# Order of the first loads, of one weight split and of two small preparations in a fused attention and expert kernel

## The chip, the cores and the metric

The kernel runs on one core of one Trainium2 chip. The metric is the device time of one execution in microseconds. Before the change it is 847.42 us, the median of 3 runs (846.95 to 848.21).

## What is computed

The reference first does attention over 4 batches, 8 heads, 576 positions, 64 columns a head. A position sees only a band behind it: heads 0 to 3 the last 32 positions, heads 4 to 7 every fourth of the last 128. Its result x, 2304 tokens by 512, goes through 4 experts that are all computed and added with weights:

```
scores = q @ k.T / sqrt(64); scores = where(mask, scores, -1e9)
attn = exp(scores - max); attn = attn / (sum(attn) + 1e-9)
x = (attn @ v), heads side by side                # 2304 x 512
p = domain_probs / (domain_probs.sum(-1) + 1e-9)  # 2304 x 4
out = sum over e of p[:, e] * (relu(x @ w1[e]) @ w2[e])   # 512 -> 1024 -> 512
```

## The kernel before

Attention is cut into 24 steps of two groups each, 192 positions of one head pair a group. A step goes through stages: `s_qk` (scores, TensorE, line 308), `s_max` (VectorE), `s_sub` (GpSimd), `s_exp` (ScalarE), `s_sum` (VectorE), `s_norm` (GpSimd), `s_tr` (transposes, TensorE, line 369) and `s_av` (products with v, TensorE, line 389). The main loop runs in rounds n (line 831). In the first part a round does scores of one step, the v products of the step three before it and the transposes of the step two before it, in this order on TensorE. Steps 0 to 4 start in rounds 0 to 4, steps 5 to 9 in rounds 8 to 12, the others from round 16 on. `START` is round 7, the round of step 4's v products; `OPEN` is round 15. Until `START` each round ends with three or four dummy matmuls (`dummies`, line 759), which keep TensorE at work.

The experts are cut into 16 units u of 256 hidden columns. All products are in float32r, and operands are split into a high and a low part: `split` (line 128) lets ScalarE write the high part (line 129) and VectorE or GpSimd the low part (line 126), so a product is high-high, low-high, high-low (line 427 for the first layer, line 530 for the second). Units 0 and 1 of the first block of 768 tokens are done plainly (`plain`, in two halves of tokens), from round 7 on with two items of `experts` a round: a round with the first two products (A11 and A21 with B11), one with the other two (A12 and A22 with B21), then the second layer's three tiles (`mm2`), and the same for unit 1. `mm2` adds to the accumulator with the experts' shares `pn`, which `weigh` makes (transposes on TensorE, line 724, then VectorE, lines 727 to 735). All other units take a scheme with fewer products (`mm1_a`, `mm1_b`) that needs sums of w1 and of x.

What prepares operands stands in a list `queue`: `prepare` adds a generator, `step` runs the first one up to its next yield, and `need` runs it to the end at once. In rounds 8 to 14 low parts are held back until the next round begins or something is needed. `x_part` splits a part of x, `w1_split` the blocks of w1, `w2_late` the two halves of w2 (for unit 1 the low part is on GpSimd).

Loads are issued by SyncE in the order of the list `loads` (line 809). At each round's start `load_ready` issues from the list's head as long as `ready` allows; a load that is not ready holds up the ones behind it, except that w2 is passed over. A tile that reuses a place makes SyncE wait for the place's last reader, and what is behind it in SyncE's queue waits too. A "fence" is a memset of one column of the tile on VectorE, for which the transfer then has to wait; it holds SyncE until VectorE has come to that point of its own queue. There are three places for q/k pairs (`QKB`) and four for v (`VB`). Before the change q/k 3 and 4 and v 4 use room in the tile `lent`, which is the first accumulator's, so that all five steps' q, k and v and w1 0 are issued without waiting; q/k 5 is fenced at round 6 (`n > half`). v_s, q_s and k_s are the tiles in their own places; both w1 and w2 land in tiles called r.

Of the kernel before, what the change touches and what calls it, by code (L numbers as in the profile page):

```python
# [8 lines left out]
F32 = mybir.dt.float32  # L9
F32R = mybir.dt.float32r  # L10
# [3 lines left out]
WINDOW = 32  # L14
# [4 lines left out]
GB = 6  # L19
GS = GB // 2  # L20
GW = GB * QB
PACE = 10
GAP = 3
QKB = 3
VB = 4
# [24 lines left out]
def kernel(  # L50
# [11 lines left out]
    nc = tc.nc  # L62
# [3 lines left out]
    NT, DM = out.shape  # L66
# [3 lines left out]
    FU = 256  # L70
    FPE = F // FU
    NU = E * FPE
    TB = 768
# [60 lines left out]
    def w1_split(u):  # L134

        r = raw1[u]
        gh = wp.tile([128, 3, 2, 128], F32R, tag="g1h", name="g1h", bufs=2)
        gl = wp.tile([128, 3, 2, 128], F32R, tag="g1l", name="g1l", bufs=2)
        a11, a12 = r[:, 0:2, 0:128], r[:, 2:4, 0:128]
        a21, a22 = r[:, 0:2, 128:256], r[:, 2:4, 128:256]  # L140
        for i, a in enumerate((a11, a12, a22)):
            split(gh[:, i], gl[:, i], a, nc.gpsimd if u else nc.vector)
            a_op[u, ("A11", "A12", "A22")[i]] = (gh[:, i], gl[:, i])
            yield
        if u < 2:
            ah, al = (
                fp.tile([128, TH], F32R, tag=t, name=t)[:, :FU].rearrange("p (c f) -> p c f", c=2)
                for t in (("hh12", "hl12"), ("u2", "s5"))[u]
            )
            split(ah, al, a21, nc.gpsimd if u else nc.vector)  # L150
            a_op[u, "A21"] = (ah, al)

    def w1_sums(u):

# [85 lines left out]
    def attention(ap, xrp, pa):  # L240
# [22 lines left out]
                ap=[row, (two.offset - one.offset, 2), col],  # L263
            )

        lent = fp.tile([128, TB // 128, DM], F32, tag="acc_0", name="lent")
        room = [lent.rearrange("p t d -> p (t d)")]

        def take(*shape):
            size = shape[0] * shape[1]  # L270
            t, room[0] = room[0][:, :size], room[0][:, size:]
            return t.rearrange("p (a b) -> p a b", a=shape[0])

        def load_qk(gs, k_queue, apart, fence):
            if apart:
                q_s, k_s = take(2, GW), take(2, GW + WINDOW)
            else:
                q_s = ap.tile([128, 2, GW], F32, tag="q", name="q_s", bufs=QKB)
                k_s = ap.tile([128, 2, GW + WINDOW], F32, tag="k", name="k_s", bufs=QKB)
            if fence:  # L280
                nc.vector.memset(q_s[:, 0, :1], 0.0)
            nc.sync.dma_start(out=q_s, in_=both(qT, gs, GW))
            k_queue.dma_start(out=k_s, in_=both(kT, gs, GW + WINDOW))
            for k, g in enumerate(gs):
                qk_t[g] = (q_s[:, k], k_s[:, k])

        def load_v(n, gs, apart):
            if apart:
                t = take(2, GB * 64).rearrange("p j (i d) -> p j i d", i=GB)
            else:  # L290
                t = ap.tile([128, 2, GB, 64], F32, tag="v", name="v_s", bufs=VB)
            for k, (b, p, gi) in enumerate(gs):
                nc.sync.dma_start(
                    out=t[KB * k:KB * (k + 1)], in_=vw[b, p][:, :, gi * GB:(gi + 1) * GB, :]
                )
            v_of[n] = t
# [216 lines left out]
    def mm2(k, first, last, half, cs=None):  # L513
        u, m = k
        e = u // FPE % E
        if first and m not in acc_t:
            if m == NBL - 1:
                pools["late"]()
            acc_t[m] = pools["acc"].tile([128, TB // 128, DM], F32, tag=f"acc_{m}", name=f"acc_{m}")
        for i in range(TH // 128):  # L520
            at = half * (TH // 128) + i
            tt = m * (TB // 128) + at
            acc = acc_t[m][:, at, :]
            po = pools["m2"].tile([128, 512], F32, tag="m2", name="m2")

            cs = cs or (range(2) if half == 0 else (1, 0))
            for n, (c, low) in enumerate([(c, low) for low in range(2) for c in cs]):
                h = h_t[k, f"{c + 1}{half + 1}"][low][:, i * 128:(i + 1) * 128]
                for x, w in enumerate(w2_op[u, c][:2 - low]):
                    nc.tensor.matmul(  # L530
                        po, h, w, start=(n == 0 and x == 0), stop=(n == 3)
                    )
            if first:
                nc.vector.tensor_scalar(
                    out=acc, in0=po, scalar1=pn[:, tt, e:e + 1], scalar2=None, op0=ALU.mult
                )
            else:
                nc.vector.scalar_tensor_tensor(  # L538
                    out=acc, in0=po, scalar=pn[:, tt, e:e + 1], in1=acc,
                    op0=ALU.mult, op1=ALU.add,  # L540
                )
            if last:
                nc.sync.dma_start(out=out[tt * 128:(tt + 1) * 128, :], in_=acc)
            yield
# [98 lines left out]
    with tc.manual_schedule():  # L643
# [131 lines left out]
        for n, i, names in (  # L775
# [9 lines left out]
        qk_done = av_done = 0  # L785
        shares = []
        ready = {"w2": lambda u: u < 1 or (u - 1, 1) in w2_op}
        half = needed[0] + 1
        ready["qk"] = lambda m: (
            m < half  # L790
            or n > half and qk_done > (m - half if m < half + QKB else m - QKB)
        )
        ready["v"] = lambda m: (
            m <= VB or av_done > m - VB - (m <= 2 * VB) and (m <= needed[1] or m <= qk_done)
        )

        def load(what, m):
            if what == "qk":
                load_qk(steps[m], nc.sync if m else nc.scalar, QKB <= m < half, m == half)
            elif what == "v":  # L800
                load_v(m, steps[m], m == VB)
            elif what == "masks":
                load_masks()
            elif what == "probs":
                shares.append(load_probs())
            else:
                (fetch_w1 if what == "w1" else fetch_w2)(m)

        loads = [
# [21 lines left out]
        for n in range(at(len(steps) - 1) + 5):  # L831
            load_ready()
            if START < n < OPEN:
                flush()
                holding.add(n)
                step()
            else:
                flush()
                holding.clear()
            for k, order in enumerate(stages):  # L840
                for stage, after in order:
                    m = step_at.get(n - after, -1)
                    if m >= 0 and k == (m > needed[1]):
                        stage(m, steps[m])
                        av_done += stage == order[(1, 2)[k]][0]
            if n in step_at:
                qk_done += 1
            for i, names in when.get(n, ()):
                for name in names:
                    of = first_x if i < 2 else later  # L850
                    if name is None or name == "T2":
                        prepare(x_sums, i, of=of)
                    if name is not None:
                        prepare(x_part, i, name.upper(), of=of)
            place = 0 if n <= START or n >= OPEN else len(queue)
            queue[place:place] = first_x
            first_x.clear()
            if n == 6:
                prepare(w1_split, 0)
            if n == START:  # L860
                prepare(w2_late, 0)
                prepare(w1_split, 1)
            if n == START + 2:
                weigh(shares[0])
            if n == START + 5:
                prepare(w2_late, 1, soon=True)
            if n == OPEN:
                gate.add("open")
            if n < START:
                dummies(FILL if n in step_at else FILL + 1)  # L870
                step()
                if n > 4:
                    step()
                    step()
                continue
            if "open" not in gate:
                for _ in range(2):
                    if next(ffn) == "idle":
                        dummies(2)
                step()  # L880
                continue
            for _ in range(PACE if n in step_at else 4):
                full = next(ffn)
                step()
                if n <= OPEN + 1:
                    step()
                if len(queue) > 8:
                    step()
                elif len(queue) < 5 and not full:
                    step(later)  # L890
# [62 lines left out]
```

## Time and profile before

| | us |
|---|---|
| median of 3 runs | 847.42 |
| profiled execution | 849.45 |
| its span, first to last instruction | 847.6 |
| TensorE busy (matmuls) | 826.9 |
| VectorE busy | 479.7 |
| GpSimd busy | 386.4 |
| ScalarE busy | 314.9 |

The mean granted TensorE clock over the span is 0.986. A granted clock of 1.00 is 2.4 GHz and 0.50 is 1.2 GHz. In the rows, PE is TensorE's matmuls, PEld its weight loads, DVE VectorE, ACT ScalarE, POOL GpSimd, SP SyncE; L389 is line 389; a q behind an engine's name is its queue, which issues and waits. All times count from the span's start.

### The profile page before, as it was taken

How to read it: one execution, taken by the hardware profiler on the slowest of the kernel's cores; microseconds unless marked ns; L12 is line 12 of the kernel's file. 1: busy time of each engine (PE TensorE's matmuls, PEld its weight loads, DVE VectorE, ACT ScalarE, POOL GpSimd, SP SyncE). 2: the span in 40 equal slices, each digit the busy share in tenths (PEclk: the TensorE clock that was granted, in tenths of full speed). 3: DMA queues.
4: the chain of work that ended last, by engine and by line, in shares of the span. 5: the costliest groups of instructions: out<-in, count | busy, mean ns of one | idle time of the engine just before them, and what ended most of it. 6: DMA issues, size and time to landing. Idle time of an engine off the chain costs nothing.

```text
span 847.6 us, 15414 instructions
## 1 busy us (share of the span) xinstructions
PE 826.9 (98%) x6172; PEld 727.3 (86%) x6172; DVE 479.7 (57%) x1042; ACT 314.9 (37%) x753; POOL 386.4 (46%) x467
## 2 busy tenths in 40 slices
PE   6979999999999999999999999999999999999998
PEld 3767888888878888899899898898998998988986
DVE  4365666655586558755545545545555455455554
ACT  2433544544454444433233233242342242232321
POOL 3264667986777679831432332342341342242210
PEclk9699999999999999999999999999999999999999
DMA  8662433343233311410100100101101001010003
GB/s 229 168 192 69 136 110 124 97 128 90 89 109 94 95 50 51 135 40 26 50 26 26 51 25 26 50 26 40 35 26 50 26 26 50 25 36 16 1 26 124
DMA packets 46610, 59.15 MB, mean 70 GB/s; under 512 B 2873, under 2 KB 36025, under 8 KB 46539
## 3 DMA queue, kind: packets, MB, share of 16 engines
q1 hardware_dynamic: 46123, 57.75, 22.6%
q8 instruction: 48, 0.79, 0.4%
q10 hardware_dynamic: 416, 0.43, 0.1%
q14 instruction: 23, 0.19, 0.1%
HBM read 53.45 MB, written 4.72 MB: 69 GB/s over the span
## 4 chain that ended last, share of the span: by engine, by line
PE 91%; POOL 3%; DVE 3%; ACT 2%; issue 1%; POOLq 0%; DVEq 0%
PE m L530 45%; PE m1x L427 23%; PE m1y L427 17%; PE po L389 2%; PE wt L759 1%; PE sc L308 1%; PE pt L369 1%; POOL w2l L126 1%; POOL sm L336 1%; DVE acc L538 1%; DVE sm L322 0%; POOL xl_T L126 0%; ACT hh L445 0%; POOL g2l L126 0%; ACT sm L343 0%
## 5 line engine op out<-in xcount | busy, mean ns | idle before, releaser
L538 DVE SCALAR_TENSOR_TENSOR acc<-m,pn,acc 128x512 f32<-128x512 f32 x270 | 201.8, 749 | 136.4 <-PE m L530 136.3
L530 PE MATMUL m<-w2h,hh 128*128 128x512 f32 x576 | 228.0, 396 | 3.9 <-ACT w2h L129 1.2
L530 PE MATMUL m<-w2l,hh 128*128 128x512 f32 x576 | 226.3, 393 | 2.2 <-POOL w2l L126 2.2
L126 POOL TENSOR_TENSOR g2l<-r,g2h 128x256 fp32r<-128x256 f32 x116 | 84.6, 762 | 214.8 <-PE m L530 212.5
L530 PE MATMUL m<-w2h,hl 128*128 128x512 f32 x576 | 179.2, 392 | 0.0
L445 ACT ACTIVATE hh<-s 128x384 fp32r<-128x384 f32 x92 | 48.4, 526 | 236.1 <-DVE s L468 183.5
L530 PEld LDWEIGHTS m<-w2h,hh 128*128 128x128 f32 x576 | 108.5, 188 | 27.3 <-DVE acc L538 4.0
L530 PEld LDWEIGHTS m<-w2h,hl 128*128 128x128 f32 x576 | 108.7, 189 | 24.0 <-DVE hl L451 0.3
L530 PEld LDWEIGHTS m<-w2l,hh 128*128 128x128 f32 x576 | 108.6, 189 | 22.7 <-POOL w2l L126 3.0
L126 POOL TENSOR_TENSOR w2l<-r,w2h 128x512 fp32r<-128x512 f32 x60 | 78.5, 1329 | 75.7 <-ACT w2h L129 75.6
L126 POOL TENSOR_TENSOR g1l<-r,g1h 128x256 fp32r<-128x256 f32 x93 | 69.9, 777 | 66.5 <-ACT g1h L129 66.4
L487 DVE TENSOR_TENSOR s<-m1x,s 128x384 f32<-128x384 f32 x46 | 25.6, 557 | 101.0 <-PE m1x L427 97.3
L478 ACT ACTIVATE u<-m1x 128x384 f32<-128x384 f32 x46 | 22.6, 492 | 150.4 <-PE m1x L427 150.4
L451 DVE SCALAR_TENSOR_TENSOR hl<-s,hh 128x384 fp32r<-128x384 f32 x92 | 53.7, 583 | 27.8 <-ACT hh L445 27.8
L427 PE MATMUL m1x<-xh_T,g2h 128*128 128x384 f32 x152 | 51.5, 339 | 0.8 <-DVE s L468 0.8
L427 PE MATMUL m1x<-xl_T,g2h 128*128 128x384 f32 x152 | 51.1, 336 | 0.0
L427 PE MATMUL m1x<-xh_T,g2l 128*128 128x384 f32 x152 | 51.0, 336 | 0.0
L129 ACT ACTIVATE g2h<-r 128x256 fp32r<-128x256 f32 x120 | 40.8, 410 | 4.8 <-POOL r L164 4.8
L427 PE MATMUL m1y<-xl_B,g2h 128*128 128x384 f32 x124 | 41.7, 336 | 0.0
L427 PE MATMUL m1y<-xh_B,g2h 128*128 128x384 f32 x124 | 41.5, 335 | 0.0
L427 PE MATMUL m1y<-xh_B,g2l 128*128 128x384 f32 x124 | 41.4, 334 | 0.0
L129 ACT ACTIVATE w2h<-r 128x512 fp32r<-128x512 f32 x64 | 39.1, 620 | 0.0
(128 smaller groups left out, 1483.5 us busy)
## 6 DMA issues: line engine op xcount, KB each, us to landing
r<-w SPq DMA_DIRECT2D x64, 512.0 KB, 3.4
v_s<-vw SPq DMA_DIRECT2D x46, 192.0 KB, 5.7
k_s<-kT SPq DMA_DIRECT2D x21, 224.0 KB, 4.9
out<-acc SPq DMA_DIRECT2D x18, 256.0 KB, 2.0
q_s<-qT SPq DMA_DIRECT2D x22, 192.0 KB, 5.0
lent<-kT SPq DMA_DIRECT2D x2, 224.0 KB
lent<-qT SPq DMA_DIRECT2D x2, 192.0 KB, 4.7
lent<-vw SPq DMA_DIRECT2D x2, 192.0 KB
```

Source lines behind the costliest of these rows:

```text
L126: lo_eng.tensor_tensor(out=lo, in0=src, in1=hi.bitcast(F32), op=ALU.subtract)
L129: nc.scalar.activation(out=hi, in_=src, func=AF.Copy)
L308: nc.tensor.matmul(banks[swap][o:o + QB, i * KB:(i + 1) * KB], q_s[h, c0:c0 + QB], k_s[h, c0:c0 + KB], start=True, stop=True, skip_group_c ...
L336: nc.gpsimd.tensor_tensor(out=sm, in0=sm, in1=nm.unsqueeze(2).to_broadcast([128, 2 * GS, KB]), op=ALU.subtract,)
L389: nc.tensor.matmul(po[k][64 * j:64 * j + 64, o:o + QB], v_s[rows, j, 2 * i + half, :], ts_[rows, c:c + QB], start=True, stop=True,)
L427: nc.tensor.matmul(bank, w[:, k], x[:, k], start=(first and k == 0 and i == 0), stop=(last and k == 1 and i == 2), skip_group_check=True,)
L445: nc.scalar.activation(out=hi, in_=src, func=AF.Relu)
L451: nc.vector.scalar_tensor_tensor(out=lo, in0=src, scalar=0.0, in1=hi.bitcast(F32), op0=ALU.max, op1=ALU.subtract)
L478: nc.scalar.activation(out=u2, in_=x, func=AF.Copy)
L487: nc.vector.tensor_tensor(out=s5, in0=x, in1=s5, op=ALU.add)
L530: nc.tensor.matmul(po, h, w, start=(n == 0 and x == 0), stop=(n == 3))
L538: nc.vector.scalar_tensor_tensor(out=acc, in0=po, scalar=pn[:, tt, e:e + 1], in1=acc, op0=ALU.mult, op1=ALU.add,)
```

## The change

The first half's q, k and v go into their own rotating places, `lent` is gone, and `ready` follows the number of steps done (`qk_done`, `av_done`). The second v comes behind q/k 3 and 4 in the order in which loads get ready, v 0 comes ahead of q/k 3, v 3 (the fourth) is fenced at round 3 and q/k 5 at round 5 instead of 6. `w1_split` splits A21 as the second of four instead of the last, with a step of its own. `weigh` runs in round `START + 1` instead of `START + 2`, and unit 1's `w2_late` is put at the queue's head in round `START + 4` instead of `START + 5`.

```diff
@@ w1_split
-        for i, a in enumerate((a11, a12, a22)):
+        for i, (n, a) in enumerate((("A11", a11), ("A12", a12), ("A22", a22))):
             split(gh[:, i], gl[:, i], a, nc.gpsimd if u else nc.vector)
-            a_op[u, ("A11", "A12", "A22")[i]] = (gh[:, i], gl[:, i])
+            a_op[u, n] = (gh[:, i], gl[:, i])
             yield
-        if u < 2:
...
+            if u < 2 and i == 0:
...
+                split(ah, al, a21, nc.gpsimd if u else nc.vector)
+                a_op[u, "A21"] = (ah, al)
+                yield
@@ load_qk, load_v
-            if apart:
-                q_s, k_s = take(2, GW), take(2, GW + WINDOW)
-            else:
-                q_s = ap.tile([128, 2, GW], F32, tag="q", name="q_s", bufs=QKB)
-                k_s = ap.tile([128, 2, GW + WINDOW], F32, tag="k", name="k_s", bufs=QKB)
+            q_s = ap.tile([128, 2, GW], F32, tag="q", name="q_s", bufs=QKB)
             if fence:
                 nc.vector.memset(q_s[:, 0, :1], 0.0)
+            k_s = ap.tile([128, 2, GW + WINDOW], F32, tag="k", name="k_s", bufs=QKB)
...
+            t = ap.tile([128, 2, GB, 64], F32, tag="v", name="v_s", bufs=VB)
+            if fence:
+                nc.vector.memset(t[:, 0, 0, :1], 0.0)
@@ main
-        half = needed[0] + 1
-        ready["qk"] = lambda m: (
-            m < half
-            or n > half and qk_done > (m - half if m < half + QKB else m - QKB)
-        )
+        ready["qk"] = lambda m: m < qk_done + QKB and (m != needed[0] + 1 or n >= m)
         ready["v"] = lambda m: (
-            m <= VB or av_done > m - VB - (m <= 2 * VB) and (m <= needed[1] or m <= qk_done)
+            m < av_done + VB and (m <= needed[1] or m <= qk_done) and (m != VB - 1 or n >= m)
         )
...
-                load_qk(steps[m], nc.sync if m else nc.scalar, QKB <= m < half, m == half)
+                load_qk(steps[m], nc.sync if m else nc.scalar, m == needed[0] + 1)
...
-                load_v(m, steps[m], m == VB)
+                load_v(m, steps[m], m == VB - 1)
...
-            ("qk", 0), ("masks", 0), ("qk", 1), ("qk", 2), ("qk", 3), ("v", 0), ("qk", 4),
+            ("qk", 0), ("masks", 0), ("qk", 1), ("qk", 2), ("v", 0), ("qk", 3), ("qk", 4),
             ("v", 1), ("v", 2), ("v", 3), ("w1", 0), ("v", 4), ("qk", 5), ("probs", 0),
...
-            if n == START + 2:
+            if n == START + 1:
                 weigh(shares[0])
-            if n == START + 5:
+            if n == START + 4:
                 prepare(w2_late, 1, soon=True)
```

## Rows read from the trace of the kernel before

**Rows 1.** The page: engine busy times, and the DMA queues (packets, MB, share).
```profile
PE 826.9 (98%) x6172; PEld 727.3 (86%) x6172; DVE 479.7 (57%) x1042; ACT 314.9 (37%) x753; POOL 386.4 (46%) x467
...
q8 instruction: 48, 0.79, 0.4%
```

**Rows 2.** Waits of TensorE, whole span: us in total, times, longest us.
```profile
PE po L389 <- issue: 4.3, 2, 4.1
PE m L530 <- POOL w2l L126: 2.2, 2, 1.7
...
PE m L530 <- ACT w2h L129: 1.2, 1, 1.2
...
PE m L530 <- DVE acc L534: 1.0, 1, 1.0
```

**Rows 3.** Stretches: busy us (instructions) per engine, granted clock, DMA share, GB/s.
```profile
16.17:20.26 4.09, 0.00 (x0) 0.00 (x0) 2.05 (x15) 0.00 (x0) 1.66 (x2) 0.90 0.66 164
20.26:32.34 12.08, 12.08 (x181) 7.74 (x180) 3.06 (x8) 5.27 (x15) 1.83 (x2) 0.50 0.24 75
32.34:36.92 4.58, 4.24 (x16) 3.45 (x12) 2.59 (x4) 3.13 (x8) 1.01 (x1) 0.54 1.05 310
...
56.35:62.57 6.22, 2.81 (x6) 1.32 (x6) 1.57 (x2) 1.67 (x4) 4.56 (x4) 0.83 0.29 81
62.57:68.74 6.17, 6.17 (x65) 5.00 (x64) 3.35 (x7) 1.46 (x4) 1.78 (x2) 0.62 0.97 292
```

**Rows 4.** Timeline of TensorE's matmuls, 13 to 21 us: start, us, instructions.
```profile
13.01 0.78 PE L389 MATMUL po<-pts,v_s 64*64 64x32 f32 x40 [0.18 <-issue]
...
15.50 0.67 PE L389 MATMUL po<-pts,v_s 64*64 64x32 f32 x32
20.26 0.65 PE L389 MATMUL po<-pts,v_s 64*64 64x32 f32 x16 [4.09 <-issue]
```

**Rows 5.** DMA view: 0 to 10.3, 10 to 11, 0 to 17.4, 17 to 18, 23 to 24.
```profile
DMA packets 2822, 2.67 MB, mean 259 GB/s; under 512 B 193, under 2 KB 2822, under 8 KB 2822
...
q8 instruction: 1, 0.02, 7.3%
...
DMA packets 4376, 4.58 MB, mean 263 GB/s; under 512 B 322, under 2 KB 4375, under 8 KB 4375
...
q8 instruction: 1, 0.02, 8.5%
...
q8 instruction: 1, 0.02, 5.5%
```

**Rows 6.** Timeline of SyncE's queue, 7 to 29 us: DMA issues.
```profile
7.12 4.77 SPq L293 DMA_DIRECT2D v_s<-vw  x6
11.93 0.59 SPq L107 DMA_DIRECT2D r<-w  x1
...
27.88 0.37 SPq L282 DMA_DIRECT2D q_s<-qT  x1
```

**Rows 7.** Timeline of TensorE's matmuls, 5 to 16 us: scores and a transpose.
```profile
5.31 0.84 PE L308 MATMUL sc<-k_s,q_s 64*32 64x64 f32 x48
...
6.84 0.72 PE L308 MATMUL sc<-k_s,q_s 64*32 64x64 f32 x48
...
10.73 0.55 PE L369 MATMUL pt<-ident,sm 128*128 128x128 f32 x3 [1.76 <-POOL sm L358]
...
11.86 0.72 PE L308 MATMUL sc<-lent 64*32 64x64 f32 x48
...
14.85 0.72 PE L308 MATMUL sc<-lent 64*32 64x64 f32 x48
```

**Rows 8.** Timeline of GpSimd, 57 to 66 us.
```profile
57.16 1.01 POOL L126 TENSOR_TENSOR xl_B<-xr,xh_B 128x384 fp32r<-128x384 f32 x1
58.12 2.81 POOL L126 TENSOR_TENSOR w2l<-r,w2h 128x512 fp32r<-128x512 f32 x2
65.53 0.83 POOL L358 TENSOR_TENSOR sm<-sm,rc 128x384 f32<-128x384 f32 x1 [4.59 <-DVE rc L353]
```

More of the change, by code (lines that the diff above doesn't have):

```diff
@@ L140, in w1_split @@
         a21, a22 = r[:, 0:2, 128:256], r[:, 2:4, 128:256]
-        for i, a in enumerate((a11, a12, a22)):
+        for i, (n, a) in enumerate((("A11", a11), ("A12", a12), ("A22", a22))):
             split(gh[:, i], gl[:, i], a, nc.gpsimd if u else nc.vector)
-            a_op[u, ("A11", "A12", "A22")[i]] = (gh[:, i], gl[:, i])
+            a_op[u, n] = (gh[:, i], gl[:, i])
             yield
-        if u < 2:
-            ah, al = (
-                fp.tile([128, TH], F32R, tag=t, name=t)[:, :FU].rearrange("p (c f) -> p c f", c=2)
-                for t in (("hh12", "hl12"), ("u2", "s5"))[u]
-            )
-            split(ah, al, a21, nc.gpsimd if u else nc.vector)
-            a_op[u, "A21"] = (ah, al)
+            if u < 2 and i == 0:
+                ah, al = (
+                    fp.tile([128, TH], F32R, tag=t, name=t)[:, :FU].rearrange(
+                        "p (c f) -> p c f", c=2
+                    )
+                    for t in (("hh12", "hl12"), ("u2", "s5"))[u]
+                )
+                split(ah, al, a21, nc.gpsimd if u else nc.vector)
+                a_op[u, "A21"] = (ah, al)
+                yield
     def w1_sums(u):
@@ L264, in both, with load_qk @@
             )
[L266 to L274, printed above, removed]
-            if apart:
-                q_s, k_s = take(2, GW), take(2, GW + WINDOW)
-            else:
-                q_s = ap.tile([128, 2, GW], F32, tag="q", name="q_s", bufs=QKB)
-                k_s = ap.tile([128, 2, GW + WINDOW], F32, tag="k", name="k_s", bufs=QKB)
+        def load_qk(gs, k_queue, fence):
+            q_s = ap.tile([128, 2, GW], F32, tag="q", name="q_s", bufs=QKB)
             if fence:
                 nc.vector.memset(q_s[:, 0, :1], 0.0)
+            k_s = ap.tile([128, 2, GW + WINDOW], F32, tag="k", name="k_s", bufs=QKB)
             nc.sync.dma_start(out=q_s, in_=both(qT, gs, GW))
@@ L285, in load_qk, with load_v @@
                 qk_t[g] = (q_s[:, k], k_s[:, k])
[L287 to L291, printed above, removed]
+        def load_v(n, gs, fence):
+            t = ap.tile([128, 2, GB, 64], F32, tag="v", name="v_s", bufs=VB)
+            if fence:
+                nc.vector.memset(t[:, 0, 0, :1], 0.0)
             for k, (b, p, gi) in enumerate(gs):
@@ L518, in mm2 @@
                 pools["late"]()
-            acc_t[m] = pools["acc"].tile([128, TB // 128, DM], F32, tag=f"acc_{m}", name=f"acc_{m}")
+            acc_t[m] = pools["acc"].tile([128, TB // 128, DM], F32, name=f"acc_{m}")
         for i in range(TH // 128):
@@ L787 @@
         ready = {"w2": lambda u: u < 1 or (u - 1, 1) in w2_op}
-        half = needed[0] + 1
-        ready["qk"] = lambda m: (
-            m < half
-            or n > half and qk_done > (m - half if m < half + QKB else m - QKB)
-        )
+        ready["qk"] = lambda m: m < qk_done + QKB and (m != needed[0] + 1 or n >= m)
         ready["v"] = lambda m: (
-            m <= VB or av_done > m - VB - (m <= 2 * VB) and (m <= needed[1] or m <= qk_done)
+            m < av_done + VB and (m <= needed[1] or m <= qk_done) and (m != VB - 1 or n >= m)
         )
```

## The prediction

> **What bounds the kernel now.** I read the page first. TensorE is busy 98% of the span [rows 1], so the time is its own work plus the few places where it waits or runs slowly; anything that leaves it idle or half-clocked early moves the end one for one. The list of TensorE's waits comes next [rows 2]: the largest is 4.1 us ahead of an attention product (line 389) with no releaser, named "issue"; then come two waits for the low part of unit 1's w2 (2.2 us), one for its high part (1.2) and one for the first accumulator (1.0). The table of stretches puts them in place [rows 3]. From 16.17 to 20.26 TensorE does nothing. From 20.26 to 32.34 it is busy for all 12.08 us at a granted clock of 0.50, which is the lower level, 1.2 GHz; the clock was at the upper level before the gap and fell in it. It is back in the next stretch. From 56.35 to 62.57 TensorE is busy for only 2.81 of 6.22 us, the clock falls again, and the stretch to 68.74 has a mean of 0.62. So the first 70 us hold two holes, each with a tail at half clock, and the change touches what stands around both.
>
> What is the first hole? TensorE's timeline shows it in the middle of one step's value products: 32 matmuls of 48, the gap, 16 more [rows 4]. Both halves of that step's v had been read before the gap, so it is no data wait. From the short "issue" gap before 13.01 to the large one TensorE issues 40 products, three transposes, three dummies, 48 scores [rows 7] and 32 products, 126 matmuls and as many weight loads, some 252 instructions. The page's instruction queue q8 brings 48 packets of together 0.79 MB [rows 1], one per 257 of TensorE's 12,344 instructions. I read the hole as TensorE out of instructions, at the end of such a block. The packet that ends it runs in 17 to 18 us [rows 5], and TensorE resumes at 20.26.
>
> Why so late? By 10.3 us 2.67 MB had moved, and the packet before started there; by 17.4 us it was 4.58 MB [rows 5]. From the tile shapes a q/k pair is 0.43 MB, a v pair 0.39, masks 0.20, one w1 tile 0.52. Five q/k pairs, masks and the first v, all that SyncE had issued by 7.1 us [rows 6], make 2.72 MB. With three more v pairs, w1 0 (11.93) and part of the last v, right behind it, it is about 4.6. Twice an instruction packet starts when the bytes issued some 3 to 5 us before it are through: it seems to stand in line behind them.
>
> **The change, part by part.** All sums are against the profiled execution, 849.45 us (span 847.6 and 1.85 around it). That lies 2.03 above the median of 847.42, and I take savings off the median.
>
> *The order of the loads.* q/k pairs 3 and 4 now reuse the places of pairs 0 and 1, so SyncE waits for the score blocks at 5.31 and 6.84 to end [rows 7], and v 1, v 2 stand behind that; v 3 waits for a memset on VectorE ahead of the fourth scores; w1 0 and v 4 follow. SyncE takes some 0.4 us to issue a q or k transfer (27.88) and 0.8 a v half (4.77 for six) [rows 6]. That gives: pair 3 issued at 6.2 to 7, pair 4 to 8.4, v 1 and v 2 to 11.6, v 3 at 11.9 to 13.5, w1 0 after that. Nothing of it is late for its reader. At (4.58-2.67)/7.1 = 0.27 MB/us pair 3 (2.3 MB in line) is through near 9 and pair 4 (2.7) near 10.4, their score blocks start at 11.86 and 14.85 [rows 7], and v 1 (3.1 MB) is through near 12 for a reader at 15.50. The memset costs VectorE one tiny operation; behind it stand only the scores, which come later.
>
> When TensorE asks for the block (12 to 13 us), 3.5 to 3.9 MB are in line rather than 4.4 or more. At 0.27 MB/us the packet starts at 13.4 to 14.9 instead of about 17.4, so 2.5 to 4 us sooner, and the 4.09 us hole shrinks to 0.1 to 1.6. I take 0.9: **-3.2** (from -4.1 to -2.4).
>
> *The clock.* With a hole of 0.9 us I expect the clock to stay up, as it did over the 1.76 us wait before 10.73 [rows 7]. The two rounds and a half in 20.26 to 32.34 then run at full clock. Halving all of the 12.08 busy us gives -6.0, the best end. The other end is the softmax chain: a round with scores took 2.99 at full clock (11.86 to 14.85) [rows 7], so 1.4 for the cut round, twice 2.99 and 0.9 for the last products make 8.3, and -3.8. The rounds in question have no scores; at 2.6 each the stretch is 7.5 us: **-4.6**. The two expert products in 32.34 to 36.92 hold 4.24 busy us at 0.54, so 2.3 at full clock. 0.34 of the stretch is idle, ahead of A21's product; splitting A21 second, on ScalarE and VectorE a round sooner, hides that behind the attention rounds, and if that cover is gone the 0.34 returns. 4.58 becomes 2.3: **-2.3** (from -2.6 to -1.9).
>
> *What TensorE runs into when it is ten microseconds early.* The second batch of loads (fenced at round 5 instead of 6) is issued from about 18.4, when VectorE is through round 4, not from 27.88 [rows 6]. Instruction blocks now stand behind it while TensorE drains them sooner. No row shows a wait there. Below it is 0; the upper bound is the hole itself, 4.1. By the same line-up I get blocks landing 0 to 1 us late at two or three places; I take **+2.0**.
>
> *Shares a round sooner.* Four transposes, a copy, and four small operations on VectorE move ahead of the first hidden layers' low parts. The 1.0 us wait for the first accumulator [rows 2] can go; but VectorE then does w2's low part, scores, shares and two hidden parts in a row. Between -1.0 and the same the other way; I take **0**.
>
> *Unit 1's w2 a round sooner.* GpSimd does this low part in 2.81 us, behind an x part of 1.01 us that starts at 57.16 [rows 8], and TensorE reads it at once. After the change its first half is through a round earlier, and its second, some 1.4 us, follows the softmax step that GpSimd leaves at 57.16: 58.6 rather than 60.9. Of 3.41 idle us in 56.35 to 62.57 some 1.6 remain. That is -1.8, and -0.5 for the clock in that stretch (2.81 busy at 0.83): **-2.3** (-3.9 if no wait is left, -0.5 if the w2 tile arrives late). With the wait halved I expect no second fall: 6.17 busy us at 0.62 are 3.8, **-2.3** (0 if it falls all the same). ScalarE's and GpSimd's x parts of chunk 0 come two steps later in turn: two of 1.01 us, hidden in GpSimd's idle time of 4.59 us before 65.53 [rows 8]; **+0.3**, at most +2.0.
>
> The sum: -3.2 -4.6 -2.3 +2.0 +0 -2.3 -2.3 +0.3 = -12.4, so 847.4 - 12.4 = **835.0**. All best ends (-4.1 -6.0 -2.6 +0 -1.0 -3.9 -2.3 +0) give -19.9 or 827.5, all bad ends (-2.4 -3.8 -1.9 +4.1 +1.0 -0.5 +0 +2.0) -1.5 or 846; as they hardly come together, the likeliest case alone runs from 829 to 842.
>
> **The rivals.**
>
> *The hole stays.* If an instruction packet does not stand behind data, the order of the data changes nothing: TensorE stops at the same place for 4.1 us and the clock falls. For this speaks that the bytes ahead were only bracketed, and that the packet of 23 to 24 us came about 3 us after TensorE resumed although the queues were empty [rows 5]; against it, the two starts that fit the line. Then A21's wait (0.34 idle and its tail at half clock, 0.6) and the second hole's -2.3 and -2.3 remain: 842. A page of the Trainium skill says just this: "DMA: Bandwidth & Descriptors", section "Queues, rings and completion order", has each DMA engine take turns between its queues packet by packet, so a lone instruction packet would be served at once. By that rule the result would be this rival's. The trace bears it out poorly (a start at 17.4 for a block asked for near 13), so it has 0.2.
>
> *The hole shrinks and the clock falls all the same.* A hole of 1.6 to 2.4 us plus waits in the softmax chain could be idle enough; the fall after 56.35 came with waits for w2 none of which was longer than 1.7 us [rows 2, 3]. Then only the hole's -2.4, A21's -0.6 and the second hole's -4.6 come: 840.
>
> *The hole moves.* This is the slower one. At 20 to 40 us the second batch, 3.1 MB, is issued at once, and TensorE's next blocks are asked for behind it. If one of them starts more than about 2 us after TensorE has used up the block before it, the clock falls in the middle of full expert work, where half clock costs half of the time: over 16 us, as long as it stayed low the first time (20.26 to past 32.34 and the tail), 8 us, and 4.1 for the hole. A residue of 1.6 in the first hole and the loss of the second hole's -4.6 to the same stall go with it: -10.1 +0.7 +4.1 +8 = +2.7, so 850. For it: 2.7 MB issued ahead put the first packet at 10.3, some 3 us after SyncE had issued them [rows 5, 6]. Against it: the batch is issued in three waits (for places), not in one.
>
> *It does not do what it says.* Gains early are given back because a later resource, GpSimd's x parts or a w2 load, sets the pace by 100 us: 847.
>
> **How the numbers follow.** Forecast 0.50 (835), hole stays 0.19 (842), clock falls 0.13 (840), hole moves 0.11 (850), given back 0.07 (847). 829 to 845.5 holds the forecast and the first two rivals nearly whole, about 0.8. A measurement of this kernel can tell 0.2%, 1.7 us, from no change: faster than 845.7 is 0.82, within 0.07, slower 0.11.
>
> **What would show it.** Right: the "issue" wait before line 389's products under 2 us, the instruction packet of that block starting before 15.5, granted clock 1.00 through 20 to 32, first expert product near 24.5 rather than 32.3, no wait over 1.2 us for w2's low part. The order of the loads is refuted if the packet still starts near 17.4; the clock step if the clock falls with a hole under 2 us; the part on w2 if TensorE still waits 3 us there. A new "issue" wait between 25 and 45 would be the third rival.

## The result and the profile after

The changed kernel takes 837.14 us (median of 4 executions, 834.86 to 839.03); the kernel before, run beside it, 847.18 (846.40 to 848.21). The ratio is 0.988, with a 95% interval from 0.985 to 0.991: 10.0 us faster. The profiled execution took 837.8 us with a span of 836.0, so span against span it is 11.6 us shorter. Line numbers of the changed kernel are 9 lower at the products: line 380 answers to 389, 360 to 369, 418 to 427, 521 to 530.

The page of the changed kernel, TensorE's busy time and granted clock:

```profile
PE 817.9 (98%) x6172; PEld 720.3 (86%) x6172; DVE 478.5 (57%) x1043; ACT 314.7 (38%) x753; POOL 386.3 (46%) x467
...
PEclk9999999999999999999999999999999999999999
```

The clock row of the kernel before:

```profile
PEclk9699999999999999999999999999999999999999
```

The number of matmuls is unchanged, VectorE has one instruction more, and the clock row no longer has the dip in its second slice. Of TensorE's waits over the whole span (us in total, times, longest) these lines answer to [rows 2]:

```profile
PE pt L360 <- issue: 2.1, 1, 2.1
...
PE m L521 <- ACT hh L436: 1.4, 3, 0.7
...
PE po L380 <- issue: 1.3, 1, 1.3
PE m L521 <- DVE acc L529: 1.2, 2, 0.8
PE m1x L418 <- DVE s L459: 1.1, 1, 1.1
...
PE m L521 <- POOL w2l L126: 0.9, 1, 0.9
...
PE m1y L418 <- issue: 0.6, 1, 0.6
```

The wait of 4.1 us before the products with v is 1.3. The wait for w2's high part is gone, that for its low part is 0.9 instead of 2.2. The wait for the accumulator at line 534 is gone too; the one at L529 stood in the kernel before as well. Two more rows of before:

```profile
PE m L530 <- DVE acc L538: 1.2, 2, 0.8
...
PE m L530 <- ACT hh L445: 0.3, 1, 0.3
```

New are a wait of 2.1 us without a releaser before a transpose and one of 0.6 before a first-layer product; the waits for hidden parts on ScalarE grew from 0.3 to 1.4.

The stretches of [rows 3], in the changed kernel, with a later one (columns as there):

```profile
16.17:20.26 4.09, 2.88 (x74) 2.16 (x74) 2.41 (x13) 1.84 (x6) 1.69 (x3) 1.00 1.07 229
20.26:32.34 12.08, 9.46 (x181) 7.12 (x178) 6.55 (x24) 6.44 (x18) 3.57 (x4) 1.00 1.08 265
32.34:36.92 4.58, 4.47 (x81) 3.37 (x89) 4.26 (x21) 2.50 (x7) 2.67 (x5) 1.00 1.08 224
36.92:53.00 16.08, 14.46 (x340) 11.90 (x329) 10.83 (x54) 7.98 (x20) 11.28 (x13) 1.00 0.72 212
```

The granted clock is 1.00 everywhere; before, TensorE did nothing in the first of them, and the next two had 0.50 and 0.54. The DMA share, which had sunk to 0.24 in the second, is above 1: the next batch of loads now runs here.

TensorE's timeline at the places that matter (start, us, instructions, idle before):

```profile
15.46 0.67 PE L380 MATMUL po<-pts,v_s 64*64 64x32 f32 x32
17.38 0.43 PE L380 MATMUL po<-pts,v_s 64*64 64x32 f32 x16 [1.25 <-issue]
...
24.51 0.33 PE L360 MATMUL pt<-ident,sm 128*128 128x128 f32 x1 [2.13 <-issue]
...
26.47 0.44 PE L418 MATMUL m1x<-xh_B,g1h 128*128 128x384 f32 x1
...
48.74 0.50 PE L521 MATMUL m<-w2h,hh 128*128 128x512 f32 x1 [0.45 <-ACT hh L436]
50.19 0.51 PE L521 MATMUL m<-w2l,hh 128*128 128x512 f32 x1 [0.95 <-POOL w2l L126]
...
73.83 0.50 PE L521 MATMUL m<-w2h,hh 128*128 128x512 f32 x1 [0.70 <-ACT hh L436]
74.82 0.50 PE L521 MATMUL m<-w2h,hh 128*128 128x512 f32 x1 [0.26 <-ACT hh L436]
...
83.34 0.44 PE L418 MATMUL m1x<-xh_T,g2h 128*128 128x384 f32 x1 [1.14 <-DVE s L459]
```

The first of these lines starts where its partner in [rows 4] does, and the stop falls after the same 32 of 48 products, as it would at the end of an instruction block. But it ends at 17.38 instead of 20.26.

Both kernels issue the same number of matmuls, 6172, in nearly the same order (the shares' four transposes move), so the start of one instruction in the two traces gives the lead at that point. Seven of them, and the end:

| instruction | before | after | lead |
|---|---|---|---|
| last 16 products after the first hole | 20.26 | 17.38 | 2.88 |
| first expert product | 32.34 | 26.47 | 5.87 |
| scores after the first two expert products | 36.93 | 28.75 | 8.18 |
| unit 1's last first-layer products (m1y, high part of B) | 55.04 | 46.54 | 8.50 |
| first v products after unit 1's first w2 round | 62.57 | 51.09 | 11.48 |
| first x part product behind that | 72.86 | 59.27 | 13.59 |
| first product with g2 | 95.25 | 83.34 | 11.91 |
| end of the span | 847.6 | 836.0 | 11.6 |

So 13.6 us were gained by 59 us, and 1.7 of them are given back between 59 and 83. From there to the end the two kernels run alike.

### The profile page after: what moved, and what is told of

Its sections match the earlier page's. It is cut to its first block, busy times and chain, and to the rows that moved or that the text cites. A ratio compares the mean times of both kernels' runs of the same rounds, so it can differ in the third digit from the quotient of the medians.

```text
span 836.0 us, 15418 instructions
## 1 busy us (share of the span) xinstructions
PE 817.9 (98%) x6172; PEld 720.3 (86%) x6172; DVE 478.5 (57%) x1043; ACT 314.7 (38%) x753; POOL 386.3 (46%) x467
## 4 chain that ended last, share of the span: by engine, by line
PE 92%; POOL 3%; DVE 2%; ACT 2%; issue 1%; POOLq 0%; DVEq 0%
PE m L521 45%; PE m1x L418 24%; PE m1y L418 17%; PE po L380 2%; PE sc L299 1%; PE pt L360 1%; PE wt L750 1%; POOL xl_T L126 1%; DVE acc L529 1%; POOL g1l L126 1%; ACT hh L436 1%; POOL w2l L126 0%; POOL g2l L126 0%; DVE sm L313 0%; ACT xh_T L129 0%
## 5 line engine op out<-in xcount | busy, mean ns | idle before, releaser
L529 DVE SCALAR_TENSOR_TENSOR acc<-m,pn,acc 128x512 f32<-128x512 f32 x270 | 201.8, 749 | 132.8 <-PE m L521 132.6
```

What stands on the lines that cost most here:

```text
L529: nc.vector.scalar_tensor_tensor(out=acc, in0=po, scalar=pn[:, tt, e:e + 1], in1=acc, op0=ALU.mult, op1=ALU.add,)
```

## The experiments

Runs e1 to e4, e5 to e8 and e9 to e12 shared a chip each, with the kernel before on it: 848.54, 847.79 and 847.08 (medians of 17, 11 and 11). The theory: instruction blocks of TensorE stand in line behind the data that was issued before them, so the loads' order sets the hole; a small hole keeps the clock up; the preparations remove the rest. The main rivals: instruction packets take turns with data and don't wait for it; the clock falls whatever the hole's size; the gain comes from the preparations alone.

**The loads alone, and the preparations alone.** e1 is the changed kernel with `w1_split` as before and the old rounds for the shares and w2:

```diff
-            if n == START + 1:
+            if n == START + 2:
                 weigh(shares[0])
-            if n == START + 4:
+            if n == START + 5:
                 prepare(w2_late, 1, soon=True)
```

> The changed kernel with A21 split last again, the shares at START + 2 and unit 1's w2 at START + 5 again: the change's loads alone. Theory (an instruction block stands in line behind the bytes issued before it): the order of the loads alone shrinks the first hole from 4.1 to about 1.2 us and keeps the clock up there, so the first expert product starts near 26.5 us rather than 32.3; the second hole stays as before, 3 to 3.4 us without work and a fall of the clock behind it. 839 to 841 us. Rival (turns: instruction packets do not stand behind data, and the gain is from the preparations): the hole stays at 4 us and the time at 847.

e2 is the kernel before with the new order of splits, shares and w2, its loads untouched.

> The kernel before with only A21 second, the shares and unit 1's w2 a round sooner; loads as before. Theory: first hole 4.1 us and half clock behind it as before; the second hole loses 2 to 3 us and, if the clock then stays up, 2 more: 841 to 843 us. Rival (turns): this is where the gain comes from, 837 to 838. If the w2 tile is what TensorE waits for rather than GpSimd's place in the order, 846 to 847.

Measured: e1 842.87 (841.37 to 843.66), ratio 0.993 [0.9916, 0.9945]; e2 843.35 (841.44 to 846.45), ratio 0.994 [0.9924, 0.996]. Either half brings some 5 us, 5.7 and 5.2; their sum of 10.9 lies between the two measurements of the whole, 10.0 above and 11.7 in e5. Both times are above what was expected (839 to 841, 841 to 843). In e1's waits the first hole is short and all of w2's stay:

```profile
PE m L518 <- POOL w2l L126: 2.2, 2, 1.7
PE pt L357 <- issue: 1.9, 1, 1.9
...
PE po L377 <- issue: 1.7, 1, 1.7
...
PE m L518 <- ACT w2h L129: 1.2, 1, 1.2
PE m L518 <- DVE acc L522: 1.1, 1, 1.1
```

In e1 the clock stays up to 55 us and falls only with the w2 waits (0.50 from 55.13 to 61.96). In e2 the first hole is the old one:

```profile
PE po L392 <- issue: 4.1, 1, 4.1
```

So the preparations don't touch the hole, and the loads don't touch w2. But part of e2's lead is the clock's. Behind this hole it came back after 3.4 us, where it stayed low until 36.5 us in the kernel before:

```profile
21.04:24.46 3.42, 3.42 (x61) 2.18 (x57) 0.91 (x3) 1.45 (x4) 0.05 (x1) 0.50 0.02 5
24.46:34.70 10.24, 8.69 (x195) 6.81 (x190) 3.55 (x7) 5.95 (x17) 2.79 (x3) 1.00 0.50 153
```

From the hole's end to the first expert product e2 takes 29.03 - 20.83 = 8.20 us instead of 12.08, in a stretch in which TensorE waits for nothing. No edit of e2 explains these 3.9 us, so how much of its 5.2 is the preparations' own is not shown, and that the halves add up proves little. e1 holds something else. Its timeline at A21's product:

```profile
28.74 0.44 PE L415 MATMUL m1y<-xh_B,hh 128*128 128x384 f32 x1 [0.51 <-ACT hh L129]
29.85 0.44 PE L415 MATMUL m1y<-xh_B,hl 128*128 128x384 f32 x1 [0.67 <-DVE hl L126]
```

TensorE waits 1.18 us for A21, where the kernel before is idle for 0.34 in that stretch [rows 3]: at half clock TensorE came to it more slowly, and ScalarE and VectorE nearly kept up.

**The line of bytes, first test.** e3 adds a load of 0.52 MB that nobody reads, on SyncE behind v 2:

```diff
-            ("v", 1), ("v", 2), ("v", 3), ("w1", 0), ...
+            ("v", 1), ("v", 2), ("extra", 0), ("v", 3), ("w1", 0), ...
```

> The changed kernel with one load more, 0.52 MB into the first accumulator's place, issued between v 2 and v 3; nobody reads it. Theory (line): at 0.27 MB a us the instruction packet of the first hole starts 1.9 us later, near 16.8 instead of 14.9, the hole grows from 1.25 to about 3.1 us, and the clock falls in it as before the change: 841 to 846 us. Rival (turns): the packet stays near 14.9, the hole at 1.25, the time at 837.

Measured: 839.58 (838.3 to 841.33), ratio 0.9895 [0.9877, 0.9913]. The packet came at 15.2 instead of 14.9 and the hole was 2.1 instead of 1.25; half clock from 18.15 to 21.56. The time is below the 841 to 846 expected. The direction of the hole is right, its size is not (3.1 was expected), and the trace says why: v 3 was issued at 11.93, behind the extra, and fell behind the packet. About 4.02 MB stood ahead instead of the 3.8 + 0.52 = 4.3 meant, so the added load pushed another out of the line. That alone doesn't separate the theories well; e12 does.

**The smallest cut of the line.** e4 is the kernel before with one edit, the fence on the fourth v:

```diff
+            if fence:
+                nc.vector.memset(t[:, 0, 0, :1], 0.0)
```

with `ready["v"]` holding v 3 until round 3.

> The kernel before, q/k 3 and 4 and v 4 still in the lent tile, with only the fourth v fenced at round 3, so that v 3, w1 0 and v 4 are issued from about 11.9 us on. Theory (line): of the bytes ahead of the block only those of w1 0 and part of the v's go; 3.5 to 3.9 MB in line, the packet at 14 to 15.5 us, a hole of 0.3 to 1.8, the clock up: 838 to 840 us with the second hole as before. If it takes the own places and their waits, or if only the total in the first 18 us counts: 847.

Measured: 845.22 (842.86 to 848.65), ratio 0.9967 [0.9951, 0.9982], 3.3 us faster, and not the 838 to 840 expected. The packet and the hole came as expected:

```profile
15.36 0.66 PE L391 MATMUL po<-pts,v_s 64*64 64x32 f32 x28 [0.36 <-DMA v_s<-vw]
17.05 0.43 PE L391 MATMUL po<-pts,v_s 64*64 64x32 f32 x16 [1.04 <-issue]
```

but the clock fell:

```profile
0.00:17.76 17.76, 13.13 (x366) 7.77 (x367) 9.04 (x73) 4.99 (x11) 7.93 (x16) 1.00 0.97 260
17.76:24.59 6.83, 6.83 (x108) 4.15 (x106) 1.96 (x5) 3.06 (x9) 2.05 (x3) 0.50 0.21 39
24.59:40.00 15.41, 13.22 (x250) 10.24 (x242) 8.99 (x41) 7.86 (x21) 5.44 (x7) 1.00 1.00 254
40.00:55.31 15.31, 11.12 (x234) 8.89 (x232) 10.71 (x52) 6.77 (x16) 9.80 (x12) 1.00 0.75 212
55.31:62.14 6.83, 6.47 (x62) 4.74 (x61) 2.59 (x6) 1.46 (x4) 2.25 (x3) 0.50 0.69 223
```

A hole of 1.04 us, less than the changed kernel's 1.25, was followed by 6.83 us at half clock. So the step "a hole of about 1 us keeps the clock up" is no law. In e4 scores at 34.85 waited 1.0 us for data besides, with the second batch of loads still fenced at round 6 as before the change, and products at 15.36 waited 0.4.

**The changed kernel again.** e5 is the changed kernel, unaltered.

> The changed kernel itself once more, beside the three that follow, since its executions spread over 4 us. Theory (line): packets start when the bytes issued ahead of them are through, so holes of 1 to 2 us near 17 and 22 us come again; how much of the clock is lost differs from execution to execution. About 0.988 of the time before: 837 to 839 us.

Measured: 836.07 (835.14 to 837.74), ratio 0.9866 [0.9849, 0.9883]. In its profile the holes are 1.5 and 0.8 us. The mean clock over the span was 0.997 to 1.0 in all eight executions of this kernel; in the kernel before it was 0.981 to 0.992 on this chip. So the second hole, 2.1 in one and 0.8 in the other, is a matter of one execution.

**The second batch later.** e6 fences q/k 5 at round 6, as before the change:

```diff
-        ... and (m != needed[0] + 1 or n >= m)
+        ... and (m != needed[0] + 1 or n > m)
```

> The changed kernel with q/k 5 fenced at round 6 instead of 5, so that the second batch is issued from about 20.5 us instead of 17.9. Theory (line): the packet that starts at 21.75 in the changed kernel, behind q/k 5, then has only the first batch ahead (4.8 MB) and starts near 19.5; the hole of 2.1 us ahead of the last transposes before the experts goes, the one of 0.6 at 32 may grow to 1; 835 to 837 us. Rival: the later batch makes scores or weights wait instead, no gain or up to 3 us slower than the changed kernel.

Measured: 838.23 (837.83 to 842.15), ratio 0.9887 [0.987, 0.9903]. The second hole is gone as expected, its packet running at 19.7 instead of 21.75, and a wait for data stands in its place:

```profile
PE sc L299 <- DMA k_s<-kT: 5.5, 2, 4.1
```

The profiled execution's clock was at 0.50 from 34.53 to 41.36 after that. So the outcome is the rival's. In the changed kernel the batch holds up instructions; issued later, it comes late itself.

**One part taken back at a time.** e7 puts w2 back to START + 5, e8 the shares back to START + 2, e9 A21's split back to the end of `w1_split`; all else is the changed kernel.

> The changed kernel with unit 1's w2 put at START + 5 again. Theory: TensorE waits for w2's parts for 3 to 3.4 us near 50 us and the clock falls for some us behind it: 3 to 5 us slower than the changed kernel, 840 to 843; and what the changed kernel gives back between 73 and 83 us (1.2 to 1.5 us, x parts two steps later) is not given back. Rival (data late or GpSimd's order does not matter): within 1 us of the changed kernel.

> The changed kernel with the shares at START + 2 again. Theory of the prediction: no difference, the wait of about 1 us for the first accumulator comes back and as much of the wait for the hidden layers' low parts goes; within 1 us of the changed kernel. Rival: the shares on VectorE ahead of the hidden parts cost nothing and the accumulator wait is pure gain: 1 us slower than the changed kernel.

> The changed kernel with A21 split last again. Theory: TensorE waits again before A21's product in the first expert round, 0.7 to 1.2 us as with the loads alone, nothing else moves: 0.7 to 1.5 us slower than the changed kernel, 837 to 838. Rival (hidden anyway): the same time.

| without | median (range) | ratio | what came back in the trace |
|---|---|---|---|
| w2 sooner (e7) | 838.98 (837.79 to 843.52) | 0.9908 [0.9887, 0.9928] | waits 1.2, 1.7 and 0.5 for w2; clock 0.50 from 49.83 to 56.66 |
| shares sooner (e8) | 837.67 (836.52 to 839.97) | 0.9885 [0.9869, 0.9901] | the accumulator's wait of 1.08 |
| A21 second (e9) | 838.51 (836.49 to 840.59) | 0.9893 [0.9874, 0.9912] | waits 0.50 and 0.67 for A21 |

Against the changed kernel's ratios, 0.988 [0.9851, 0.9908] here and 0.9866 in e5, the intervals overlap the wider one. Against e5, on the same chip, e7's does not, though its time is below the 840 to 843 expected; for the other two parts the times alone settle nothing. The rows say more. e8's line:

```profile
37.20 0.50 PE L521 MATMUL m<-w2h,hh 128*128 128x512 f32 x1 [1.08 <-DVE acc L525]
```

In e7's trace the first w2 product of unit 1 starts at 46.81, 0.85 ahead of the changed kernel's, in spite of a wait of 1.22 there; its first x part product, at 62.20, is 2.93 behind. But its product with g2 comes at 84.60, against 83.34: of the 2.93 only 1.26 are left. What the w2 edit gains at 50 us is in good part given back by 83.

e9 shows how far the clock varies: its first loads are the changed kernel's, its hole was 1.15, and the clock fell:

```profile
17.13 0.43 PE L377 MATMUL po<-pts,v_s 64*64 64x32 f32 x16 [1.15 <-issue]
...
0.00:18.15 18.15, 13.56 (x368) 7.97 (x369) 9.05 (x74) 5.29 (x12) 7.94 (x16) 1.00 0.93 259
18.15:28.39 10.24, 10.24 (x161) 6.31 (x159) 3.05 (x7) 4.71 (x13) 2.05 (x3) 0.50 1.03 279
```

Of its six executions the two with a mean clock of 0.992 and 0.993 took 840.2 and 840.6 us, the four with 0.997 to 1.0 took 836.5 to 839.1.

**What is given back.** e10 adds one step of the queue in rounds 13 and 14, so that the x parts are split as early in turn as before the change:

```diff
+                if n > START + 5:
+                    step()
```

> The changed kernel with one preparation step more in rounds 13 and 14 (two in all), so that x parts of chunk 0 that came two steps later are split where GpSimd idles (54 to 65 us). Theory: what the changed kernel gives back between 73 and 84 us (1.2 to 1.7 us, waits for ScalarE's hidden parts and for a sum on VectorE) goes: 1 to 1.7 us faster than the changed kernel, 834 to 836. Rival: those waits have another cause, no difference; or the parts ahead of the last attention products make TensorE wait at 59 us, up to 1 us slower.

Measured: 837.0 (834.34 to 840.36), ratio 0.9871 [0.9845, 0.9896], not the 834 to 836 expected and not to be told from the changed kernel by time. In its profile the clock is at 0.50 from 51.66 to 55.07 and its first x part product comes 1.83 us after the changed kernel's (61.10); but the product with g2 comes at 83.82, only 0.48 behind. It regains 1.35 us there, and its rows show where most of it is:

```profile
76.00 0.50 PE L521 MATMUL m<-w2h,hh 128*128 128x512 f32 x1 [0.28 <-ACT hh L436]
...
83.82 0.45 PE L418 MATMUL m1x<-xh_T,g2h 128*128 128x384 f32 x1 [0.79 <-DVE s L459]
```

1.07 us of waits, against 0.70 + 0.26 + 1.14 = 2.10 in the changed kernel; the kernel before has the same 0.28 and 0.79. GpSimd's rows of the changed kernel show the cause, three x parts in a row ahead of the sums of w1 (lines 163 to 169, from 70.28 on):

```profile
65.15 2.96 POOL L126 TENSOR_TENSOR xl_T<-xr,xh_T 128x384 fp32r<-128x384 f32 x3 [10.80 <-ACT xh_T L129]
68.08 2.12 POOL L126 TENSOR_TENSOR g1l<-r,g1h 128x256 fp32r<-128x256 f32 x3
```

ScalarE then waits longer for these sums, 5.85 us in the changed kernel and 4.76 before, and writes the hidden part for TensorE behind them:

```profile
72.67 0.72 ACT L129 ACTIVATE g2h<-r 128x256 fp32r<-128x256 f32 x2 [5.85 <-POOL r L167]
73.30 0.47 ACT L436 ACTIVATE hh<-m1x 128x384 fp32r<-128x384 f32 x1
```

```profile
84.31 1.03 ACT L129 ACTIVATE g2h<-r 128x256 fp32r<-128x256 f32 x3 [4.76 <-POOL r L164]
```

In e10 two of the three x parts run from 59.60 on, in GpSimd's idle time.

**Moving the second batch past VectorE.** e11 lets GpSimd write q/k 5's fence and loads q/k 6 ahead of w1 1:

```diff
-                nc.vector.memset(q_s[:, 0, :1], 0.0)
+                nc.gpsimd.memset(q_s[:, 0, :1], 0.0)
```

> The changed kernel with q/k 5 fenced at round 5 by GpSimd's memset instead of VectorE's (some 1 us later, near 18.9 us, after the packet has been asked for) and q/k 6 ahead of w1 1. Theory (line): the packet of the second hole has only the first batch ahead of it, starts near 19.6 instead of 20.9 to 21.75, and the hole of 0.8 to 2.1 us shrinks under 0.5; the scores of step 6 do not wait as they did with the fence at 6, since their load comes 0.5 MB sooner: 0.5 to 1.5 us faster than the changed kernel. Rival: data is late instead (scores or w1 1), 0 to 2 us slower.

Measured: 838.7 (835.89 to 840.81), ratio 0.9893 [0.9872, 0.9915]. The time is not the 0.5 to 1.5 us gain expected. The hole at the transpose is 0.8 (its packet at 20.0 instead of 21.75), but it is 0.8 in e5 and e7 too, which leave this load alone, so no gain from the edit is shown there. The next block is late instead:

```profile
32.70 0.45 PE L418 MATMUL m1y<-xh_B,g1h 128*128 128x384 f32 x1 [2.79 <-issue]
```

with 3.4 us at half clock after it. At that place the wait was 0.6 in the changed kernel and at most 0.3 in e5, e7 and e8, so this block comes late in e11.

**The line of bytes, second test.** e12 adds the same 0.52 MB, which nobody reads, on ScalarE's queue in round 2, so that SyncE's order stays:

```diff
+            if n == 2:
+                t = fp.tile([128, TB // 128, DM], F32, name="acc_0")
+                nc.scalar.dma_start(out=t[:, :2, :], in_=...)
```

> The changed kernel with one load more, 0.52 MB that nobody reads, issued by ScalarE's queue near 10 us, so that SyncE's issues keep their times. Theory (line, whatever queue the bytes come from): 4.3 MB are ahead of the block instead of 3.7 to 3.8, its packet starts 1.5 to 2 us later, near 16.6, and the first hole is 2.8 to 3.3 us instead of 1.1 to 1.5; 1.5 us slower or more, depending on the clock. Rival (turns between queues): packet and hole as in the changed kernel.

Measured: 840.34 (836.47 to 842.76), ratio 0.991 [0.9882, 0.9939]. The DMA view of e12 from 0 to 16.0 us, and its instruction row from 15 to 16.02:

```profile
DMA packets 3828, 4.17 MB, mean 261 GB/s; under 512 B 290, under 2 KB 3575, under 8 KB 3827
...
q8 instruction: 1, 0.02, 7.4%
```

and TensorE's timeline:

```profile
15.32 0.67 PE L380 MATMUL po<-pts,v_s 64*64 64x32 f32 x32
18.69 0.66 PE L380 MATMUL po<-pts,v_s 64*64 64x32 f32 x16 [2.71 <-issue]
```

The packet starts at 16.0, behind 4.2 MB, where the changed kernel's starts at 14.86 behind 3.8 (3.70 MB by 14.8 us), and the hole grows by 1.46. TensorE was not later on its way (its fourth scores start at 12.06, in the changed kernel at 12.19). The load went through another engine's queue and still stood ahead of the instructions. The clock was at 0.50 from 17.87 to 34.94, as before the change.

## Why the prediction was right, step by step

The time, 837.14, lies 2.1 above the 835.0 forecast. The terms, read off the leads, are those of one execution each; they add up to 11.6 and not to the 10.0 between the medians, since the profiled execution before was 2.03 above its median:

| term | predicted | measured |
|---|---|---|
| first hole | -3.2 | -2.9 |
| rounds at full clock | -4.6 | -5.1 |
| two expert products, A21 among them | -2.3 | -2.3 |
| later blocks late | +2.0 | +2.1 |
| shares, with the wait of 0.6 at 32.45 | 0 | -0.3 |
| unit 1's w2, waits | -2.3 | -3.0 |
| no second fall | -2.3 | -2.1 |
| x parts later in turn | +0.3 | +1.7 |
| from 83 us to the end | | +0.3 |
| sum | -12.4 | -11.6 |

The rounds are 12.08 before, and 26.47 - 17.38 - 2.13 = 6.96 after. The expert products are 36.93 - 32.34 = 4.59 before and 28.75 - 26.47 = 2.28 after. All other terms are differences of neighbouring leads. That the sum came so near is in part errors that cancel: the rounds and w2 came 1.2 better, the x parts 1.4 worse.

**The line of bytes** was the step on which the first half rested, and it holds. In nine traces the first loads are the changed kernel's (it, e1, e5 to e11): the packet starts at 13.8 to 15.6 us, when 3.6 to 3.8 MB have moved, and the hole is 0.8 to 1.8; e4, with the fence alone, fits them (14.27, 3.7 MB, 1.04). With 4.0 MB (e3) the hole is 2.1, with 4.2 (e12) 2.7, with 4.6 (before and e2) 4.1. In all fourteen traces TensorE resumes 2.4 to 3.0 us after the packet's start. The changed kernel's own 14.86 lies at the late end of the 13.4 to 14.9 predicted and its hole of 1.25 within 0.1 to 1.6; among the nine, three packets and two holes lie above these ranges. The rival of packets that take turns is refuted here by e12. The Trainium skill ("DMA: Bandwidth & Descriptors", "Queues, rings and completion order") has each DMA engine alternate between its queues packet by packet; a lone instruction packet would then have been untouched by e12's extra load, and it started at 16.0, later than in any of the nine and behind some 0.4 MB more.

**The rounds** came to 6.96 us, 0.5 better than the 7.5 that 2.6 us a round had given. The first expert product is at 26.47 and not near 24.5 because of the 2.13 hole at 24.51, which is the term of later blocks. I had that term spread over two or three places; it is one, and its size varies: in e5, the same kernel, that hole is 0.8. The wait of 0.60 at 32.45 is the new "issue" wait between 25 and 45 that was named as a sign of the third rival, but it is far below that rival's 4.1, the clock did not fall behind it, and it cost nothing: from 28.75 to 46.54 the changed kernel takes 17.79 us, and e5, which has no such wait, 17.80.

**The clock** stayed up in both profiles of the changed kernel, as predicted, but not for the reason given, that the hole is short. In the other traces it stayed up behind first holes of 0.80, 0.98, 1.02, 1.08, 1.50, 1.66 and 1.77 us (e7, e6, e11, e8, e5, e1, e10) and fell behind 1.04, 1.15, 2.07 and 2.71 (e4, e9, e3, e12). The size of the hole does not order them, and by the prediction's own sign, a fall with a hole under 2 us, the step is refuted as a rule. That it came out right here is in part luck, and the second rival's chance of 0.13 was, if anything, low. Two things are common to the four that fell and absent from the others: TensorE had also waited 0.2 to 0.8 us for a load ahead of the hole, and its nine opening dummies had taken 3.46 to 3.65 us, in the others 3.83 to 4.02. No run varies either alone, so what decides stays open. In the eight executions of the changed kernel the mean clock is never below 0.997; three have 0.997 or 0.998, and e10's profile shows that 0.998 can hold a fall of 3.4 us.

**A21** was mis-sized inside a term that came out right. I gave its split 0.34 of the 2.3. e1 and e9 show that at full clock TensorE would wait 1.18 for it; the two products last 30.92 - 26.91 = 4.01 in e1, 2.28 with the split. In the kernel before, at half clock, they last 4.59, so the clock alone brings 0.6. The split alone brings as little: in e12, where A21 is second and the clock still low (a mean of 0.52), they last 35.11 - 31.07 = 4.04. Only both together bring 2.3: a wait seen while the waiting engine is slow understates the wait that stands behind it.

**The shares** were given 0, between -1.0 and +1.0. From the scores behind the first two expert products to unit 1's last first-layer products it takes 17.8 us with the shares sooner (the changed kernel, e5, e7, e10), 18.1 in the kernel before and in e1, and 19.1 in e8: 0.3 better than before, and 1.3 better than without them in the changed kernel. In e5 TensorE instead waits 0.37 and 0.41 us for a hidden part and a softmax result in that stretch, so a part of the accumulator's wait came back in another form, as the prediction had allowed for. **w2** came at 0.45 + 0.95 = 1.40 us of waits against 1.6 predicted, none over the 1.2 that I had set as the test, and the products of that stretch ran at full clock. That no second fall follows is likelier now, not sure: with w2 in its old place the clock fell in all four traces (before, e1, e4, e7), with w2 sooner in two of ten, e10 and e11, for 3.4 us each. **The x parts** are the term that was too small: +0.3 with an upper bound of +2.0, measured +1.7, of which 1.03 stands in the rows (2.10 of waits against 1.07); the rest is in no listed wait. I had GpSimd's idle time cover them; it does not, because they come into the queue after it, three in a row, ahead of the sums of w1 that ScalarE and then TensorE wait for. e10 shows it by undoing it, and e7, with w2 and so the x parts in their old turn, has the wait of 0.28 again instead of 0.70 and 0.26.

No variant beats the changed kernel beyond the spread; e10's best executions, 834.34 twice with a clock of 1.0, are the lowest seen. Whether its regained 1.35 us is real in the median stays open, as its six times spread over 6 us with the clock.

## What to carry to other kernels

When an engine stops for nothing that the profile names, look at where the instruction packets run and at how many bytes were issued ahead of them on any queue: in these traces the order and the moment of issue of loads also set when code arrives. A load that is issued long before it is needed is not free, and holding it back with a fence shortens the line; hold it back too far and it is late itself (e6) or the next block is (e11). And a wait seen beside a slow clock must be worked out anew for the fast one.

## What had not been expected of the hardware

After a like hole the clock's lower level lasts very differently: after a hole of 4.09 us it was 17 us in the kernel before (19.5 to 36.5), but 3.4 in e2 (21.04 to 24.46), though TensorE worked without a gap behind the hole in both, in the kernel before until 34.9 us; after 1.0 to 2.7 us it was nothing, 3.4, 6.8, 10.2 or 17.1. And between two executions of one kernel the same instruction block can start 0.8 us apart (20.94 in e5 and 21.75); with TensorE there 0.5 us sooner in the second, the hole was 0.8 us in the one and 2.1 in the other.
